# A gated state-space and dense kernel: other load order and warm-up at the start, due times from a table, two late output groups

## The chip, the cores and the metric

One core of one Trainium2 chip runs the kernel. The metric is the device time of one execution in microseconds, as the median of several runs. The profile is of one execution; its times are counted from the start of its span.

## The reference

For 2048 tokens x of 512 channels the output mixes two branches by a gate of each token: `g * a + (1 - g) * b`, where g is the sigmoid of the sum over channels of x times gate_w. Branch b is a dense pair of layers. Branch a is a long convolution whose 2048 taps come from 128 complex exponentials per channel; the reference does it with FFTs over 4096 points.

```python
dt = jnp.exp(log_dt)[:, None]
logdA, dB = dt * A, dt * Bc                       # 512 x 128, complex
P = jnp.exp(logdA[:, :, None] * l[None, None, :]) # l = 0 .. 2047
K = jnp.einsum("dn,dnl,dn->dl", Cc, P, dB).real
y = irfft(rfft(pad(u)) * rfft(pad(K)))[:2048] + u * Dskip   # branch a
h = gelu(x @ w1 + b1)                              # 512 -> 1792
b = h @ w2 + b2                                    # 1792 -> 512
out = g * a + (1 - g) * b
```

## The kernel before

The kernel has two parts, `front` and `conv`.

`front` runs four streams of tasks. **Dense**: the tokens go in 8 blocks of 256 (`xh`, `xlo`: each number as the sum of two of a shorter format, so that a product takes three matmuls: high by high, low by high, high by low). Each block meets the 1792 hidden columns in two passes of seven w1 tiles (`wh`, `wl`), so that there are 16 rounds, called NB. A hidden group (L904 to L906, 12 matmuls into `ph`) makes one hidden tile of 128; ACT applies the GELU and copies it to `hh`, DVE puts the rest into `hl`; an output group (L947 to L950, six matmuls, three where a step has one tile only) adds it to `acc`, one accumulator for each half of the block. A step is two hidden tiles, the fourth step of a round one: that is the last column of the pass. The second pass stores its result with an accumulating DMA on GpSimd's queue (L990). **Taps**: DVE and ACT make powers of the exponentials, 16 pieces in all; PE contracts each (L709, into `pk`), the first stage of a transform follows (L428), ACT copies its result to `sk` (L736), and SP stores it to `tk_d` in DRAM (L751), eight stores for four pieces. **Signal**: the same first stage for x, to `tu_d`. **Early**: loads of `tu_d` into rooms that become free (`den`, `loft`, `attic`, L474).

The tasks of all four streams go into a planner (`Plan.run`), which writes out the order: on each engine or queue the task with the smallest due time among those that are ready by its clock. A task's due time is worked out from constants such as `T_0`, `D_H`, `K_0`. Every engine then works through its rows in that order and waits at a row whose inputs are missing; the order never changes while the kernel runs.

At the start PE does eight matmuls on a zeroed tile `dm` (`warm`, L1025), spreads `b2` and `gate_w` over the partitions with one-row matmuls (`spread`, L1029), and goes on to the first hidden group. `make_dt` loads log_dt, makes its exponential and writes it to `dt_d`; `prepare` reads it back with a broadcast DMA to `dtb` for each of four channel blocks.

`conv` is the second stage: for each of 16 steps p2u and p2k (L1140) transform signal and taps, which come from `us` and from `tk_d` (L1119), DVE multiplies them, `pa` (L1179) goes back, ACT copies to `sa`, and SP stores to `t_d`. Loads of quarters of `t_d` (L1185) bring the rows together for the last transform pb (L1295, 16 tiles of 512 columns); DVE adds each to what the dense branch left in `mos` and SP stores the output. The output products of the last round, and one group of the last column of the round before (128 tokens, copied to `odd`), are kept in the list `late`; `rest` issues them behind the loop, while the quarters travel.

Of the kernel before, what the change touches and what calls it, by code (L numbers as in the profile page):

```python
# [33 lines left out]
T_0 = 36.21  # L34
T_MLP = 409.57
K_0 = 25.82
T_KG = 357.09
U_0 = 33.4
U_GAP = 11.32
LAG = 11.52  # L40
TABLE = 21.3
D_KA = 14.92
D_KP = -48.19
D_S1 = -107.61
D_EV = -129.31
D_H = -67.42
D_LO = -64.4
PS = (2, 3, 1, 2)
N_ACC, N_H, N_PK, N_PU = PS
D_SP = 5.83  # L50
MEM = (6, 2, 5)
N_LD, N_HL, N_ST = MEM
D_XS = 6.62
DOTS_AT = (0, 1, 7, 14, 15, 18, 20, 21)
N_WARM = 8
T_EARLY, T_LOFT, T_DEN = 347.49, 497.61, 268.21
Y_K, Y_U = 55.03, 39.32
W_MLP = (-0.0864, -0.0266, 0.0054)
W_KG = (-0.056, -0.0124, 0.0011)
W_U = (-0.025, -0.1189, 0.003)  # L60
D_MAG = -1.84
D_ROT = 0.71
D_CON = 2.06
D_PHA = -0.1
D_PRE = -2.18
D_XL = -29.86
D_COE = -3.15
D_OUT = -38.48
D_GW = 95.59
D_DT = -103.6  # L70
D_B2 = 15.56
N_LATE = 2
N_REST = 3
N_KEEP = 2
# [7 lines left out]
W_DVE = ((1, 0), (3, 0), (5, 0))  # L82

# [35 lines left out]
def constants():  # L119
# [14 lines left out]
    c1 = np.tile(np.stack([er, ei], 2).reshape(32, 64), (4, 1))  # L134

# [73 lines left out]
class Plan:  # L209
# [26 lines left out]
    def run(self):  # L236
# [8 lines left out]
        for _ in self.tasks:  # L245
# [23 lines left out]
            if p in ("SP", "GP"):  # L269
                dma = max(dma, at + 1.2) + t.done  # L270
                end = dma + 1.2
# [16 lines left out]
def gated_mix(  # L288
# [52 lines left out]
    def front(pool, psum, keep, attic, loft, den, pr):  # L341
# [57 lines left out]
        odd = keep.tile([P, 2, P], F32R, name="odd")  # L399
# [80 lines left out]
        def make_dt():  # L480
# [23 lines left out]
            move(2, lambda: nc.sync.dma_start(x, logdt.rearrange(shape, c=4)), D_DT, [], ["dt"])  # L504
# [3 lines left out]
            move(2, lambda: nc.sync.dma_start(dt_d.rearrange(shape, c=4), r), -200, ["dt"], ["dt_d"])  # L508
# [24 lines left out]
        def prepare(u, t, eb_k):  # L533
# [4 lines left out]
            move(600, lambda: nc.sync.dma_start(pr, prm[:, :, sl]), t - 20 if u else -97, [], ["pr"])  # L538
            move(
                200, lambda: nc.gpsimd.dma_start(dtb, dt_d[:, sl].to_broadcast([P, UW])), t - 20 if u else -97,  # L540
                ["dt_d"], ["dtb"], queue="GP",
            )
# [341 lines left out]
        def halves(i):  # L884
# [6 lines left out]
            k = i % N_HL  # L891
            return hh[k][:, 0:n], hl[k][:, 0:n], ("hh", k), ("hl", k)

        def hidden(i, t):
# [33 lines left out]
            act((0.75, 1.45)[nf - 1], gelu, t + D_H, ["b1"], [hk, ("h", q)], "gelu")  # L928
# [6 lines left out]
        def output(i, t):  # L935
# [4 lines left out]
            def products(s, a):  # L940
# [3 lines left out]
                for n, f in enumerate(fs):  # L944
# [4 lines left out]
                    stop = (j == 2 and n == 1) if b == NB - 2 and s else j == 3  # L949
# [4 lines left out]
            for s in range(2):  # L954
# [6 lines left out]
                if b == NB - 2 and s and j == 3:  # L961
                    for k, (z, key) in enumerate(((hi, hk), (lo, lk))):
                        pl.add(
                            "POOL", 0.3, lambda k=k, z=z: nc.gpsimd.tensor_copy(odd[:, k], z[:, 0, P:].bitcast(F32)),
                            t, [key], [("odd", k)],
                        )
                    late.append((2, odd[:, 0], odd[:, 1], wh[1][fs[0] % FH], wl[1][fs[0] % FH]))
# [26 lines left out]
        def dense():  # L994
# [6 lines left out]
                lambda: nc.gpsimd.dma_start(c1t, c1),  # L1001
# [32 lines left out]
            for q in range(1, N_ACC):  # L1034
# [4 lines left out]
            split_x(0, x, -50)  # L1039
            first = [  # L1040
                split_w(f, r, room[f][:, r], ("room", f, r), -50 + f + r * 1.5, (f, r) in W_DVE)
# [47 lines left out]
        while heap:  # L1089
# [3 lines left out]
            if t is not None:  # L1093
                heap.append((t, n, s))
        for t in pl.run():
# [4 lines left out]
    def conv(pool, ps, late, attic, loft, den, pr):  # L1100
# [116 lines left out]
        def rest(n):  # L1217

            while late and n:
# [3 lines left out]
                if first:  # L1223
                    tag, bufs = ("pk", 2) if s < 2 else ("pa1", 1)
# [53 lines left out]
        rest(15)  # L1278
# [114 lines left out]
```

## Time and profile before

| | us |
|---|---|
| runs shown, median (lowest to highest) | 510.12 (509.39 to 512.53) |
| profiled execution, its own time | 510.31 |
| its span | 508.3 |
| PE busy, 4792 instructions | 500.2 (98%) |
| DVE busy | 430.0 (85%) |
| ACT busy | 364.7 (72%) |
| GpSimd busy | 39.6 (8%) |
| moved by DMA | 107.60 MB, 212 GB/s on average |

The profile of one execution has a span, from the first to the last instruction, and the time of that execution stands beside it. A row of its views names line, engine, operation and tiles (output, arrow, inputs); "idle before" is the time in which the engine had nothing to do ahead of the row, and the name behind it is what ended that. Transfers are shown by the engine that issues them: SPq, POOLq and ACTq are the queues of SyncE, GpSimd and ScalarE.

### The profile page before, as it was taken

The numbers are of one execution on the slowest core, as the hardware profiler recorded it, in microseconds if no ns is written. First come the engines' busy times: TensorE is split into PE (matmuls) and PEld (weight loads), VectorE is DVE, ScalarE is ACT, GpSimd is POOL, SyncE is SP. The second block draws the span as 40 slices with busy tenths as digits, with TensorE's granted clock in tenths as the row PEclk, the third lists the DMA queues.
The fourth block names the chain that finished last, engine by engine and source line by source line (L and its number), as shares of the span: only waits on it lengthen the run. The fifth ranks groups of instructions, "written<-read, shape, count | busy, mean of one in ns | idle before, by whom it ended". The sixth has DMA issues, their size and how long they took to land.

```text
span 508.3 us, 12156 instructions
## 1 busy us (share of the span) xinstructions
PE 500.2 (98%) x4792; PEld 382.8 (75%) x4792; DVE 430.0 (85%) x814; ACT 364.7 (72%) x631; POOL 39.6 (8%) x80
## 2 busy tenths in 40 slices
PE   9999999999999999999998999999999999999996
PEld 6998788898989888788887898998898832222452
DVE  5797999999999999999998989999950188777546
ACT  5799997889999599999766998738634455565300
POOL 1000000000000000001020010120010000231100
PEclk9999999999999999999999999999999999999999
DMA  8977597732558642789594233951478899989997
GB/s 269 327 250 269 156 258 236 225 128 66 149 120 260 193 165 64 207 241 239 142 269 139 86 54 59 218 119 29 144 179 206 201 368 401 376 300 399 324 339 294
DMA packets 81552, 107.60 MB, mean 212 GB/s; under 512 B 39396, under 2 KB 43880, under 8 KB 80952
## 3 DMA queue, kind: packets, MB, share of 16 engines
q1 hardware_dynamic: 74936, 82.81, 51.6%
q0 software_dynamic: 6176, 21.80, 16.1%
q10 hardware_dynamic: 384, 2.23, 1.3%
q8 instruction: 37, 0.61, 0.5%
q14 instruction: 19, 0.16, 0.1%
HBM read 61.19 MB, written 45.62 MB: 210 GB/s over the span
## 4 chain that ended last, share of the span: by engine, by line
PE 74%; ACT 16%; DMA 4%; SPq 3%; issue 2%; DVE 1%; DVEq 0%; POOL 0%; ACTq 0%; POOLq 0%
PE pk L709 10%; PE ph L904 8%; PE acc L947 7%; PE ph L905 7%; PE ph L906 7%; PE acc L948 7%; PE acc L950 7%; PE p2u L1140 5%; PE p2k L1140 5%; PE pa L1179 3%; PE pb L1295 3%; ACT ph L921 2%; PE ph L428 2%; ACT L921 2%; SPq L751 1%
## 5 line engine op out<-in xcount | busy, mean ns | idle before, releaser
L904 PE MATMUL ph<-xh,wh 128*128 128x256 f32 x448 | 129.4, 289 | 0.5 <-ACT attic L446 0.5
L905 PE MATMUL ph<-xlo,wh 128*128 128x256 f32 x448 | 128.1, 286 | 1.5 <-issue 1.5
L906 PE MATMUL ph<-xh,wl 128*128 128x256 f32 x448 | 127.9, 285 | 0.0
L904 PEld LDWEIGHTS ph<-xh,wh 128*128 128x128 f32 x448 | 86.4, 193 | 9.3 <-issue 5.4
L905 PEld LDWEIGHTS ph<-xlo,wh 128*128 128x128 f32 x448 | 86.5, 193 | 3.5 <-issue 1.7
L906 PEld LDWEIGHTS ph<-xh,wl 128*128 128x128 f32 x448 | 86.4, 193 | 0.0
L947 PE MATMUL acc<-wh,hh 128*128 128x512 f32 x209 | 84.2, 403 | 0.0
L948 PE MATMUL acc<-wl,hh 128*128 128x512 f32 x209 | 82.2, 393 | 0.0
L950 PE MATMUL acc<-wh,hl 128*128 128x512 f32 x209 | 81.8, 392 | 0.0
L921 ACT ACTIVATE ph<-ph,b1t 128x256 f32<-128x256 f32 x112 | 50.4, 450 | 38.9 <-PE ph L906 37.1
L709 PE MATMUL pk<-y,den 128*32 128x64 f32 x2048 | 61.4, 290 | 0.0
L709 PEld LDWEIGHTS pk<-y,den 128*32 128x32 f32 x2048 | 57.2, 136 | 3.3 <-issue 1.8
L931 DVE TENSOR_TENSOR hl<-ph,hh 128x512 fp32r<-128x512 f32 (+1 forms) x62 | 38.3, 620 | 22.6 <-ACT hh L924 22.2
L947 PEld LDWEIGHTS acc<-wh,hh 128*128 128x128 f32 x209 | 39.3, 188 | 17.4 <-issue 7.8
L950 PEld LDWEIGHTS acc<-wh,hl 128*128 128x128 f32 x209 | 39.3, 188 | 8.8
L671 DVE TENSOR_TENSOR y<-y,ea 128x64 f32<-128x64 f32 (+4 forms) x80 | 45.4, 567 | 0.1
L948 PEld LDWEIGHTS acc<-wl,hh 128*128 128x128 f32 x209 | 39.3, 188 | 6.4
L516 DVE TENSOR_TENSOR loft<-den,zz 128x256 f32<-128x256 f32 (+2 forms) x48 | 37.4, 778 | 0.5
L517 DVE TENSOR_TENSOR loft<-den,zz 128x256 f32<-128x256 f32 (+2 forms) x48 | 37.3, 776 | 0.0
L1148 ACT COPY k<-p2k 128x512 f32<-128x512 f32 x32 | 18.7, 586 | 25.4 <-issue 10.2
L684 DVE TENSOR_TENSOR y<-y,loft 128x2048 f32<-128x2048 f32 x16 | 36.6, 2288 | 0.2
L924 ACT CAST hh<-ph 128x512 fp32r<-128x512 f32 (+1 forms) x62 | 33.0, 533 | 2.4 <-PE acc L948 0.2
(200 smaller groups left out, 875.0 us busy)
## 6 DMA issues: line engine op xcount, KB each, us to landing
tk_d<-sk SPq DMA_DIRECT2D x32, 256.0 KB, 5.0
t_d<-sa SPq DMA_DIRECT2D x32, 256.0 KB, 5.1
tu_d<-attic SPq DMA_DIRECT2D x40, 128.0 KB, 2.8
attic<-in_xt_dram SPq DMA_DIRECT2D x16, 256.0 KB, 5.4
xh_d<-xh SPq DMA_DIRECT2D x8, 512.0 KB, 4.5
xl_d<-xlo SPq DMA_DIRECT2D x8, 512.0 KB, 5.0
attic<-in_xs_dram SPq DMA_DIRECT2D x16, 256.0 KB, 5.3
out_dram<-io SPq DMA_DIRECT2D x16, 256.0 KB, 3.3
```

The lines of the kernel that those rows point to most:

```text
L516: vec(2 * m, lambda: vv.tensor_mul(t, a, br), due, [ka, *kb], [kt])
L671: nc.vector.tensor_mul(both(n, 64 - 3 * n, n), both(0, 64 - n, n), an)
L709: nc.tensor.matmul(pks[q][32 * j : 32 * j + 32, :, gg], x[:, r, :, ch], y[:, r, :, ch], start=(r == 0), stop=(r == 1), skip_group_check=True,)
L904: nc.tensor.matmul(p, h, xh[xk][:, d], start=(d == 0), stop=False)
L905: nc.tensor.matmul(p, h, xlo[xk][:, d], start=False, stop=False)
L906: nc.tensor.matmul(p, lo, xh[xk][:, d], start=False, stop=(d == 3))
L921: nc.scalar.activation(phs[q][:, n], phs[q][:, n], AF.Gelu_apprx_tanh, bias=b1t[:, f : f + 1])
L931: nc.vector.tensor_sub(lo, phs[q][:, 0:nf], hi.bitcast(F32))
L947: nc.tensor.matmul(a, h, wh[1][w], start=start, stop=False, skip_group_check=seeded)
L948: nc.tensor.matmul(a, h, wl[1][w], start=False, stop=False, skip_group_check=seeded)
L950: nc.tensor.matmul(a, l, wh[1][w], start=False, stop=stop, skip_group_check=seeded)
L1140: nc.tensor.matmul(out[64 * i : 64 * i + 64], w, x, start=True, stop=True)
```

## The change

Four things change together.

1. Due times: a string of numbers, one for each task, replaces the due times that the constants gave. The constants change too, but where a task has a due time the table's holds.
2. The start: SP loads the first half of x, then w1's first tile, then x's second half. log_dt comes by GpSimd's queue. The first `dtb` is no longer read back from DRAM: a new constant (`some`, beside `c1`) times dt is multiplied by ones on PE and copied by DVE. The warm-up has 12 matmuls instead of 8.
3. The last column of the last round but one goes behind the loop for both halves of the block (256 tokens). Its inputs stay in `hh` and `hl`; the GpSimd copies to `odd` go.
4. In the tail the matmuls that kept PE at work (N_KEEP, `warm`) are gone, and the last of the 16 pb tiles is done in two halves of 256 columns.

```diff
-D_KA = 14.92
+D_KA = 27.96
...
-N_WARM = 8
+N_WARM = 12
...
-N_KEEP = 2
...
+DUES = """
+2 48 1704 7 63 0 8 101 3 31 2 0 9 1 25 4 7 18 32 13 55 6 75 19 64 22 23 16 3 0 3 1 0 26 460 580 33 1539 174
...
+        for t, due in zip(pl.tasks, map(float, DUES.split()), strict=True):
+            t.due = due
         for t in pl.run():
             t.fn()
...
     c1 = np.tile(np.stack([er, ei], 2).reshape(32, 64), (4, 1))
+    some = np.arange(P)[:, None] == np.arange(P) // 4
+    c1 = np.concatenate([c1, some], 1)
...
-            move(2, lambda: nc.sync.dma_start(x, logdt.rearrange(shape, c=4)), D_DT, [], ["dt"])
+            move(2, lambda: nc.gpsimd.dma_start(x, logdt.rearrange(shape, c=4)), -300, [], ["dt"], queue="GP")
...
+            some, scaled, ones = (x4[0:32, 0, k] for k in range(3))
+            pl.add("POOL", 0.1, lambda: nc.gpsimd.memset(ones, 1.0), -190, [], ["x4"])
+            move(16, lambda: nc.gpsimd.dma_start(some, c1[0:32, 64:192]), -190, [], ["x4"], queue="GP")
...
+            mm(
+                0.4, lambda: nc.tensor.matmul(pus[1][:, 0:UW], ones, scaled, start=True, stop=True), -190,
+                ["x4"], [("pu", 1)], tiled=True,
+            )
+            vec(UW, lambda: v.tensor_copy(dtb, pus[1][:, 0:UW]), -190, [("pu", 1)], ["dtb"])
...
-                    load(xt[b, :, 2 * h : 2 * h + 2].rearrange("p a b -> p (a b)"), due)
+                    load(xt[b, :, 2 * h : 2 * h + 2].rearrange("p a b -> p (a b)"), due + 2 * h)
...
-                        -99 + f + r * 1.5, [], [("room", f, r)],
+                        -99 + f + r * D_W1 if f + r else -299, [], [("room", f, r)],
...
-                if b == NB - 2 and s and j == 3:
-                    for k, (z, key) in enumerate(((hi, hk), (lo, lk))):
...
-                    late.append((2, odd[:, 0], odd[:, 1], wh[1][fs[0] % FH], wl[1][fs[0] % FH]))
+                if b == NB - 2 and j == 3:
+                    late.append((2 + s, hi[:, 0], lo[:, 0], wh[1][fs[0] % FH], wl[1][fs[0] % FH]))
...
-        rest(15)
-        odd = pool.tile([P, D], F32, tag="v0", name="odd", bufs=2)
-        nc.scalar.mul(odd, accs[2], gate[:, 1, 13:14])
-
-        warm = ps.tile([P, D], F32, tag="pa0", name="warm", bufs=1)
-        for _ in range(N_KEEP):
-            nc.tensor.matmul(warm[0:64], mats[7][1][:, 1], zs[0], start=True, stop=True)
+        rest(16)
+        odd = [pool.tile([P, D], F32, tag=f"v{r}", name=f"odd{r}", bufs=2) for r in range(2)]
+        for r in range(2):
+            nc.scalar.mul(odd[r], accs[2 + r], gate[:, 1, 12 + r : 13 + r])
+
...
+                parts = [slice(0, D // 2), slice(D // 2, D)] if t == 15 else [slice(0, D)]
+                for cs in parts:
...
                 if m == 1 and i == 0:
-                    nc.vector.tensor_add(mos[6][:, 1], mos[6][:, 1], odd)
+                    for r in range(2):
+                        nc.vector.tensor_add(mos[6][:, r], mos[6][:, r], odd[r])
```

How the rows move is seen at three places. A number behind a name is a buffer; the lines of the changed kernel are its own.

**The start.** GpSimd before: the zeroed `dm`, the load of b2 into io_145, the ones of the spread, the load of the gate weights.

```order
L1019 MEMSET dm 128x128
L1016 DMA io_145<-in_b_dram 1x16x32
L1013 MEMSET s_106 1x128
L765 MEMSET phase 128x32
L1016 DMA io_146<-in_gw_dram 1x16x32
```

GpSimd in the changed kernel, from the same place on; x_98 holds the ones and the constant of the new broadcast, dts_149 log_dt.

```order
L571 MEMSET x_98 32x128
L1092 DMA io_144<-in_b_dram 1x16x32
L1095 MEMSET dm 128x128
L844 MEMSET phase 128x32
L1089 MEMSET s_106 1x128
L565 DMA dts_149<-in_logdt_dram 128x4
L1092 DMA io_145<-in_gw_dram 1x16x32
L572 DMA x_98<-in_c_dram 32x128
```

A memset and the load of b2 now stand ahead of dm. PE before, its first rows: warm-up, the two spreads, the first hidden group.

```order
L1025 MATMUL acc_87<-dm 128x128 x8
L1029 MATMUL acc_86<-io_145,s_106 128x512
L1029 MATMUL pu_92<-io_146,s_106 128x512
L904 MATMUL ph_88<-xh_108,wh_112 128x256
L905 MATMUL ph_88<-xlo_110,wh_112 128x256
```

PE in the changed kernel, its first rows.

```order
L1101 MATMUL acc_87<-dm 128x128 x12
L1105 MATMUL acc_86<-io_144,s_106 128x512
L985 MATMUL ph_88<-xh_108,wh_112 128x256
L986 MATMUL ph_88<-xlo_110,wh_112 128x256
L987 MATMUL ph_88<-xh_108,wl_126 128x256
```

The second spread and the new broadcast of dt (L583) stand 36 matmuls further on, behind three hidden groups:

```order
L986 MATMUL ph_90<-xlo_110,wh_116 128x256
L987 MATMUL ph_90<-xh_108,wl_130 128x256
L1105 MATMUL pu_92<-io_145,s_106 128x512
L583 MATMUL pu_93<-x_98 128x128
L985 MATMUL ph_89<-xh_108,wh_114 128x256
```

A 128-wide matmul in this format counts as two of the profile's instructions.

**The hand-over from front to conv.** SP before, from the last eight stores of sk on; den and loft are loads from tu_d, tk the first loads of `conv`.

```order
L474 DMA den<-tu_d 128x512
L751 DMA tk_d<-sk 64x16x64 x2
L474 DMA den<-tu_d 128x512
L751 DMA tk_d<-sk 64x16x64 x4
L474 DMA den<-tu_d 128x512
L751 DMA tk_d<-sk 64x16x64 x2
L474 DMA loft<-tu_d 128x512
L1119 DMA tk_4781<-tk_d 128x512
```

SP in the changed kernel at the same place.

```order
L535 DMA den<-tu_d 128x512
L830 DMA tk_d<-sk 64x16x64 x2
L535 DMA den<-tu_d 128x512
L830 DMA tk_d<-sk 64x16x64
L535 DMA loft<-tu_d 128x512
L830 DMA tk_d<-sk 64x16x64 x2
L535 DMA den<-tu_d 128x512
L830 DMA tk_d<-sk 64x16x64 x3
L1197 DMA tk_4783<-tk_d 128x512
```

Three loads stay among the stores; none stands behind them now. On PE, 141 rows of hidden and output groups (108 and 33) stand before between the last first stage and the first p2u; in the changed kernel 108 (84 and 24). ACT before, behind the copies to sk: the two results of the last round but one (io) that GpSimd's accumulating stores take.

```order
L921 ACTIVATE ph_90<-ph_90,b1t 128x256
L924 CAST hh_141<-ph_90 128x256
L977 ACTIVATE io_146<-acc_87,gate 128x512
L977 ACTIVATE io_145<-acc_86,gate 128x512
L921 ACTIVATE ph_88<-ph_88,b1t 128x256 x2
L924 CAST xh_108<-ph_88 128x512
```

ACT in the changed kernel at that place.

```order
L1005 CAST hh_141<-ph_90 128x256
L1002 ACTIVATE ph_88<-ph_88,b1t 128x256 x2
L1005 CAST xh_108<-ph_88 128x512
L1053 ACTIVATE io_145<-acc_87,gate 128x512
L1002 ACTIVATE ph_89<-ph_89,b1t 128x256 x2
L1005 CAST xh_108<-ph_89 128x512
L1053 ACTIVATE io_144<-acc_86,gate 128x512
```

Both results moved behind GELUs of the last round.

**The tail.** PE before: the last late group, the matmuls that kept it at work, the first pb tile.

```order
L1227 MATMUL acc_5485<-wh_125,odd 128x512
L1228 MATMUL acc_5485<-wl_139,odd 128x512
L1229 MATMUL acc_5485<-wh_125,odd 128x512
L1284 MATMUL warm<-z_4779,cc_5205 64x512 x2
L1295 MATMUL pb_5496<-den,g1t 64x512 x2
```

PE in the changed kernel.

```order
L1305 MATMUL acc_5487<-wh_125,hh_141 128x512
L1306 MATMUL acc_5487<-wl_139,hh_141 128x512
L1307 MATMUL acc_5487<-wh_125,hl_143 128x512
L1305 MATMUL acc_5491<-wh_125,hh_141 128x512
L1306 MATMUL acc_5491<-wl_139,hh_141 128x512
L1307 MATMUL acc_5491<-wh_125,hl_143 128x512
L1375 MATMUL pb_5501<-den,g1t 64x512 x2
```

One more late group stands there, and no matmuls of its kind to keep PE at work.

More of the change, by code (lines that the diff above doesn't have):

```diff
@@ L269, in run @@
             if p in ("SP", "GP"):
-                dma = max(dma, at + 1.2) + t.done
-                end = dma + 1.2
+                dma = max(dma, at + 1.2) + t.done * (1.5 if dma < 6.5 else 1.0)
+                end = dma + (1.2 if p == "SP" else 2.6)
                 landed[p].append(end)
@@ L537, in prepare @@
             act_due = t + D_KA
[L538 to L542, printed above, removed]
+            move(600, lambda: nc.sync.dma_start(pr, prm[:, :, sl]), t - 20 if u else D_PR, [], ["pr"])
+            if u:
+                move(
+                    200, lambda: nc.gpsimd.dma_start(dtb, dt_d[:, sl].to_broadcast([P, UW])), t - 20,
+                    ["dt_d"], ["dtb"], queue="GP",
+                )
             v = nc.vector
```

112 lines of the change are left out of this document (60 added, 52 removed), and 55 rows, old and new, of the table DUES.

## The prediction

> **What bounds the kernel now.** The sum is made against the profiled execution: its span is 508.3 us, its own time 510.31 us, so 2.0 us lie around the span; the three runs shown have a median of 510.12 us. One per cent, 5.1 us, is about what a measurement of this kernel can tell from no change. I read the page's first two parts and its chain of work first, then the waits of PE, then windows and timelines of the three places that the change touches: the start, the hand-over from the front to the convolution stage, and the tail.
>
> ```profile
> PE 500.2 (98%) x4792; PEld 382.8 (75%) x4792; DVE 430.0 (85%) x814; ACT 364.7 (72%) x631; POOL 39.6 (8%) x80
> PE   9999999999999999999998999999999999999996
> PE 74%; ACT 16%; DMA 4%; SPq 3%; issue 2%; DVE 1%; DVEq 0%; POOL 0%; ACTq 0%; POOLq 0%
> ```
>
> PE is busy in 98% of the span, and in nine tenths or more of every slice but the last, so time can only come from fewer matmuls, from a faster PE clock, or from the few places where PE waits. DVE stands second:
>
> ```profile
> 51.00:375.00 324.00, 321.31 (x3713) 278.39 (x3712) 315.92 (x601) 268.52 (x450) 22.45 (x45) 1.00 0.58 159
> ```
>
> DVE is busy for 315.92 of these 324 us: it feeds the tap stage, and a schedule that gives PE less to wait for must not ask more of DVE. The waits of PE's matmuls in the whole span are five:
>
> ```profile
> PE ph L905 <- issue: 1.5, 1, 1.5
> PE acc L1025 <- POOL dm L1019: 1.0, 1, 1.0
> PE ph L904 <- ACT attic L446: 0.5, 1, 0.5
> PE ph L428 <- ACT wh L808: 0.4, 1, 0.4
> PE ph L428 <- DVE hl L931: 0.2, 1, 0.2
> ```
>
> Without the 1.0 us of the start, 2.6 us are there to be had in the loop, and 1.5 us of them have no releaser that the profile shows.
>
> **The start.** PE runs at half its rate at first. The same matmuls, by count in two windows:
>
> ```profile
> 8.79:13.06 4.27, 4.27 (x21) 1.00 1.06 387
> 13.94:16.08 2.14, 2.14 (x21) 1.00 0.96 350
> 0.73 0.20 POOL L1019 MEMSET dm<- 128x128 f32 x1 [0.29 <-POOLq L1374]
> 0.99 3.79 PE L1025 MATMUL acc<-dm 128*128 128x128 f32 x16 [0.99 <-POOL dm L1019]
> 1.31 0.64 POOL L1016 DMA_DIRECT2D io<-in_b_dram  x1 [0.37 <-issue]
> 1.94 0.19 POOL L1013 MEMSET s<- 1x128 f32 x1
> 4.71 2.06 PE L1029 MATMUL acc<-io,s 1*128 1x512 f32 x2
> 6.57 1.91 PE L1029 MATMUL pu<-io,s 1*128 1x512 f32 x2
> 7.09 0.62 ACT L808 CAST wh<-sk 128x512 fp32r<-128x512 f32 x1 [2.05 <-DMA sk<-in_w_dram]
> 8.41 0.58 PE L904 MATMUL ph<-xh,wh 128*128 128x256 f32 x1
> ```
>
> 21 matmuls take 4.27 us before 13.06 us and 2.14 us after 13.94 us. From 8.41 us to the step between the two windows, near 13.3 us, the loop therefore loses about 2.4 us, and the full rate came after 4.9 us of dense work. The 16 warm-up matmuls (3.79 us) and the one-row matmuls behind them, which spread b2 and the gate weights, did not bring the full rate.
>
> The change issues 24 warm-up matmuls instead of 16, at the 0.213 us each that 16 in 3.4 us give: 5.1 us. But POOL now does a memset and the b2 load (0.64 us) ahead of the memset of dm on which the warm-up waits; dm takes the place that the memset behind that load has now, near 1.9 us, so the warm-up runs from about 2.2 to 7.3 us instead of from 0.99. One spread (1.9 us at half rate, 0.95 us at full) stays ahead of the first hidden group; the other goes 36 matmuls behind it. When the full rate comes decides the rest. If 4.9 us of dense work bring it, as they did above, it is there at 7.1 us, as the warm-up ends; the spread then takes 0.95 us, and the first hidden group starts at 8.2 us. If half of that work is enough (4.7 us), the rest of the warm-up goes at full rate and the group starts at 6.9 us; if the warm-up does not bring it, at 9.2 us, with half rate until about 13.3 us. I take the value that the row gives, 8.2 us. Its data come no later: w1's first piece is now the second of SP's transfers instead of the fourth. A hidden task still reads both halves of x, so "half of x" moves the loads, not the condition. On the path that is 8.41 - 8.2 = 0.2 us earlier and 2.4 us of half rate gone, less 0.95 us for the spread that came behind, 0.25 us for the new matmul that broadcasts dt (a quarter of a spread's columns), and some 0.8 us in which that matmul waits for DVE, which has a weight tile (0.7 us) and the last dt rows ahead of it: 0.6 us gained. The bounds are 2.7 us gained (6.9 us, no wait for DVE) and 2.4 us lost (9.2 us: 0.8 later, half rate 0.4 us cheaper, 1.2 us of added matmuls, the wait).
>
> [...]
>
> The earlier dt also lets DVE begin the taps sooner. That shortens DVE's chain, which is not the end's bound, and I price it at nothing as long as PE stays the busier engine.
>
> **The loop.** One output group of three matmuls leaves it for the tail. A matmul of that shape takes 0.23 us from start to start, one of a hidden group 0.12 us:
>
> ```profile
> 59.02 0.29 PE L905 MATMUL ph<-xlo,wh 128*128 128x256 f32 x1
> 59.14 0.28 PE L906 MATMUL ph<-xh,wl 128*128 128x256 f32 x1
> 382.99 0.40 PE L947 MATMUL acc<-wh,hh 128*128 128x512 f32 x1
> 383.23 0.39 PE L948 MATMUL acc<-wl,hh 128*128 128x512 f32 x1
> ```
>
> That is 0.7 us off a saturated stretch. All other instructions stay, in another order. Five output groups of the old order stand only two hidden groups (24 x 0.12 = 2.9 us) behind the hidden group whose GELU they read, one of the new; so I let 1.3 us of the 2.6 us of waits go. Bounds: all 2.6 us gone, or as much again added, since the new order was never run in this trace.
>
> **The hand-over.** Here the change costs. The taps' last first-stage products leave PE, ACT copies them to sk, SP stores them to tk_d in eight transfers, and SP loads them back as tk for the first p2k matmul:
>
> ```profile
> 382.29:402.92 20.63, 20.63 (x141) 19.11 (x141) 2.50 (x4) 9.96 (x20) 2.32 (x4) 1.00 0.84 193
> 402.92:406.41 3.49, 3.49 (x18) 1.19 (x17) 1.12 (x2) 0.95 (x3) 0.00 (x0) 1.00 0.76 214
> 382.29 2.06 ACT sk L736 x4
> 384.37 0.59 SPq L751
> 394.77 7.46 DMA tk_d<-sk
> 402.31 0.33 SPq L1119
> 406.41 4.33 PE L1140 MATMUL p2k<-tk,pr 128*64 128x512 f32 x16
> PEld p2k L1140 <- DMA tk<-tk_d: 0.4, 1, 0.4
> q0 software_dynamic: 288, 0.52, 16.3%
> ```
>
> From the first copy (382.29) to the first p2k (406.41) the transfers take 24.1 us, and PE needs as long: 20.63 us for 141 matmuls, then 3.49 us of p2u. The two end together, with a 0.4 us wait. In the new order 108 matmuls stand there, 24 hidden ones and 9 output ones fewer: 24 x 0.12 + 9 x 0.23 = 4.9 us less. PE is ready 15.7 + 3.5 = 19.2 us after the first copy. The chain of transfers is nearly the same: eight stores and three loads from tu_d (the last of the three no longer behind the stores, where it did not delay them). What differs is the two accumulating stores of the output on GpSimd's queue: they held 16.3% of the DMA time from 384 to 402.3 us, 3.0 us; in the new ACT order they follow the GELUs of the last block, so one meets the last stores and one the loads. The chain takes 21.1 us without them and 24.1 us as before; with one of two in the way I take the middle, 22.6. PE then stands still for 3.4 us (1.9 to 4.9) instead of 0.4: +3.0 us.
>
> **The tail.**
>
> ```profile
> 485.61 1.56 ACTq L1185 DMA_DIRECT2D den<-t_d  x2
> DMA to landing us min/median/max: 3.9/4.0/4.6
> 488.10 1.93 PE L1284 MATMUL warm<-z,cc 128*64 128x512 f32 x4
> 489.65 3.81 PE L1295 MATMUL pb<-den,g1t 128*64 128x512 f32 x16
> 492.47 0.68 DVE L1302 TENSOR_TENSOR loft<-loft,odd 128x512 f32<-128x512 f32 x1
> 496.25 6.76 DVE L1305 SCALAR_TENSOR_TENSOR loft<-pb,gate,loft 128x512 f32<-128x512 f32 x8
> 503.12 1.74 DVE L1305 SCALAR_TENSOR_TENSOR attic<-pb,gate,attic 128x512 f32<-128x512 f32 x3
> ```
>
> The first pb matmul starts at 489.65 us, as the quarter that ACT issued at 485.61 us lands (3.9 us). The warm matmuls (488.10, 1.93 us) fill that wait. The change takes them out and puts the 0.7 us of matmuls into the same wait: nothing moves, because the transfer ends it; should the transfer come earlier than PE, the 0.7 us would be back. The second add of odd costs DVE 0.68 us, but DVE needs 0.77 us for a tile (3.07 us for four) where PE's pace is 0.845 (6.76 us for eight), and gains 0.075 us on each of the fourteen tiles left, 1.0 us in all. The last tile in halves lets DVE begin its first half sooner, yet DVE still has the tile before it (0.77 of the 1.74 us): 0.1 us gained, at most 0.4.
>
> **The sum.** -0.6 - 0.7 - 1.3 + 3.0 - 0.1 = +0.3 us. Span 508.6 us, time 510.6 us: **no change** by this working.
>
> **The rivals.** *The transfers are in time.* If the eight stores and the loads keep up with the shorter stretch (fewer packets beside them than I count), the 3.0 us fall away and with them the old 0.4 us: 507.2 us, and with the best start (2.1 more), a loop without waits (1.3) and the last tile's 0.3 us 503.5 us. For it: one store's issue takes SP only 0.59 us when nothing is queued. Against it: 7.46 us from the last store's issue to its landing, with DMA as the chain's only holder.
>
> *PE goes cold in the hand-over (slower).* Its wait there is one gap, and the windows at the start show a PE that had to work 4.9 us before it got the full rate. If such a gap takes the rate away again, the same 4.9 us at half rate cost 2.4 us on top: 513.0 us, with the wait at its upper bound (1.5 more) 514.5 us, and with the cold start (3.0 more) 517.5 us. It decides from the gap at which the rate falls, which no row here shows, for PE never waits over 1.5 us; against it is that my gap is short. [...]
>
> *The new order stalls PE.* A table of due times for every task may put a matmul group ahead of its GELU or its weights: as much waiting again as now, +2.6 instead of -1.3, gives 514.5 us. Against it are the longer distances counted above.
>
> *It does not do what it says*: the longer warm-up does not bring the full rate, and the first group starts at 9.2 us. Then 0.6 gained becomes 2.4 lost, 513.6 us.
>
> **How the numbers follow.** No change by the sum 0.48; transfers in time 0.25; PE cold 0.12; new stalls 0.08; no early rate 0.07. The predicted time is that of the sum, 510.6. From 503.5 (the best of the second case) to 514.5 (both slow ones at their bounds) about 8 in 10 are held; I give 504.0 to 515.0. Faster by over 1% (below 505.0) needs the second case with a good start or an unstalled loop, 0.15 of its 0.25, and 0.04 of the first: 0.19. Slower by over 1% (above 515.2) needs PE cold with a cold start, stalls beside the full wait, or a cold start beside it: 0.07 + 0.04 + 0.03 = 0.14. The rest, 0.67, is within 1%.
>
> **What would show it.** Start: the first hidden matmul near 8.2 us, 0.12 us apart from the outset, and a gap ahead of the dt matmul. Loop: the waits of PE below 2.6 us. Hand-over: PE idle between p2u and p2k for 2 to 5 us, released by the load of tk; if PE is idle for less than 1 us there, the main cost is wrong. Tail: pb's first matmul still released by the load of den. I am wrong if the rate at the start is half up to 13 us, if DVE holds the last tap chunk back, or if the loop's stalls differ by more than 2.6 us.

## The result, and the profile after

The changed kernel takes 512.93 us (median of 19 runs, 511.05 to 517.81) against 510.12 us (19 runs, 508.9 to 512.53) before: ratio 1.0056, 95% interval 1.0039 to 1.0073. That is slower by 0.6%, inside the 1% that was called no change and inside the range, 2.3 us above the forecast of 510.6. The profiled execution has a span of 511.1 us, 2.8 us more than before.

The row of the engines and PE's row of the 40 slices, after the change:

```profile
PE 498.3 (98%) x4802; PEld 379.6 (74%) x4802; DVE 430.4 (84%) x817; ACT 363.6 (71%) x631; POOL 39.5 (8%) x80
PE   8999999999999999999999999999999699999995
```

PE does 1.9 us less and the span is longer: one slice, the 32nd, has fallen to 6 tenths. The waits of PE say which place that is:

```profile
PE p2k L1218 <- DMA tk<-tk_d: 3.9, 1, 3.9
PE acc L1101 <- POOL phase L844: 2.2, 1, 2.2
PE pb L1375 <- DMA den<-t_d: 0.8, 1, 0.8
PE p2k L1218 <- ACT k L1226: 0.4, 1, 0.4
PE pu L583 <- DVE x L575: 0.2, 1, 0.2
PE p2u L1218 <- DVE hl L1012: 0.2, 1, 0.2
```

No wait of the loop is left, and the hand-over has one of 3.9 us. Its rows in PE's timeline (start, duration, line, operation):

```profile
398.90 1.94 PE L1218 MATMUL p2u<-den,pr 128*64 128x512 f32 x8
...
406.82 5.97 PE L1218 MATMUL p2k<-tk,pr 128*64 128x512 f32 x16 [3.85 <-DMA tk<-tk_d]
...
415.04 1.09 PE L1257 MATMUL pa<-v,pr 64*64 64x512 f32 x8
```

And four windows around it (width, PE, PEld, DVE, ACT and POOL busy, granted clock, DMA share, GB/s):

```profile
400.71:404.12 3.41, 2.06 (x10) 0.49 (x8) 0.26 (x1) 0.00 (x0) 0.00 (x0) 1.00 0.92 167
404.12:407.53 3.41, 0.71 (x3) 0.30 (x5) 0.00 (x0) 0.00 (x0) 0.00 (x0) 1.00 0.66 191
407.53:410.94 3.41, 3.41 (x10) 1.21 (x10) 0.69 (x1) 0.59 (x1) 0.00 (x0) 0.50 1.01 314
410.94:414.36 3.42, 3.03 (x15) 0.76 (x13) 2.67 (x5) 2.48 (x5) 0.00 (x0) 1.00 1.05 382
```

PE stands still for 3.85 us before the first p2k matmul. The window that holds most of the gap has 0.71 us of work, and in the next one, 3.41 us long, PE is busy throughout at a granted clock of 0.50. The sixteen p2k matmuls take 5.97 us instead of 4.33. So the gap is paid twice, as waiting and as a half-rate window behind it: 3.41 us at half rate do the work of 1.7 us.

By stages, the two profiled executions differ so:

| stage, and where its ends are read | before | after | difference |
|---|---|---|---|
| span's start to the first p2u | 402.92 | 398.90 | -4.0 |
| first p2u to first p2k | 3.49 | 7.92 | +4.4 |
| first p2k to first pa | 6.25 | 8.22 | +2.0 |
| first pa to first pb | 77.0 | 76.9 | -0.1 |
| first pb to the span's end | 18.6 | 19.1 | +0.5 |

(Before, the first pa matmul started at 412.66 us.) The 4.0 us that PE gains ahead of p2u are given back in the next row, and the stretch with the half-rate window is 2.0 us longer (1.7 us for the window; p2k's later matmuls also wait 0.4 us for ACT). The loop in a window of the same width, before and then after:

```profile
51.00:380.00 329.00, 326.31 (x3848) 283.02 (x3847) 316.89 (x603) 269.61 (x452) 22.45 (x45) 1.00 0.59 160
```

```profile
51.00:380.00 329.00, 329.00 (x3869) 285.08 (x3871) 316.20 (x603) 265.94 (x447) 22.35 (x45) 1.00 0.57 160
8.20:11.60 3.40, 3.40 (x24) 2.66 (x23) 1.72 (x6) 2.52 (x6) 0.00 (x0) 1.00 1.06 389
```

PE's busy time rises from 326.31 to 329.00 of 329.00 us: all 2.7 us of waiting are gone. (The last row is of the start. The rate there is read from the matmuls, for the granted clock is given as 1.00 from 2.20 to 7.70 us too: the spread, which ends just ahead of the hidden group, takes 1.37 us, where it takes 1.9 to 2.1 us at half rate (the kernel before) and 1.12 at full (the second spread of this execution, at 13.40 us), so the full rate came near 8.2 us; before, it came near 13.3.) DVE has 316 to 317 us in both, and its last tap piece ends nearly where it did, before and then after:

```profile
373.89 1.21 DVE L695 TENSOR_TENSOR y<-y,loft 128x1024 f32<-128x1024 f32 x1
```

```profile
374.25 1.22 DVE L774 TENSOR_TENSOR y<-y,loft 128x1024 f32<-128x1024 f32 x1
```

That is 375.10 us before and 375.47 after. DVE could not finish sooner: a few rows earlier it waited 2.0 us for a contraction of PE, which came late in the new order.

```profile
366.71 0.17 DVE L804 TENSOR_TENSOR pk<-pk,dm 128x8 f32<-128x8 f32 x1 [2.01 <-PE pk L788]
```

Before, the same row (L725) stood at 364.33 us, with a wait of 0.27. One row of the start and one of the tail, after:

```profile
8.94 0.39 PE L985 MATMUL ph<-xh,wh 128*128 128x256 f32 x1
491.98 1.51 PE L1375 MATMUL pb<-den,g1t 128*64 128x512 f32 x6 [0.76 <-DMA den<-t_d]
```

The first hidden group starts 0.5 us later than before (8.94 instead of 8.41 us), at full rate, and pb still waits for its load. As for the hand-over: PE got ahead, the taps did not, and the first p2k needs the taps: the first copy to sk went from 382.29 to 383.25 us, and the first p2k only from 406.41 to 406.82.

### The profile page after: what moved, and what is told of

It is laid out like the page before. It is cut to its first block, busy times and chain, and to the rows that moved or that the text cites. A ratio compares the mean times of both kernels' runs of the same rounds, so it can differ in the third digit from the quotient of the medians.

```text
span 511.1 us, 12182 instructions
## 1 busy us (share of the span) xinstructions
PE 498.3 (98%) x4802; PEld 379.6 (74%) x4802; DVE 430.4 (84%) x817; ACT 363.6 (71%) x631; POOL 39.5 (8%) x80
## 4 chain that ended last, share of the span: by engine, by line
PE 90%; DMA 4%; SPq 2%; ACT 1%; issue 1%; DVE 1%; POOL 0%; DVEq 0%; ACTq 0%; POOLq 0%
PE pk L788 12%; PE acc L1028 10%; PE ph L985 10%; PE ph L987 10%; PE ph L986 10%; PE acc L1029 9%; PE acc L1031 9%; PE p2k L1218 6%; PE p2u L1218 5%; PE ph L489 3%; PE pa L1257 3%; PE pb L1375 3%; DMA tk_d<-sk 2%; SPq L830 1%; PE acc L1101 1%
## 5 line engine op out<-in xcount | busy, mean ns | idle before, releaser
L985 PE MATMUL ph<-xh,wh 128*128 128x256 f32 x448 | 127.4, 284 | 0.0
L986 PE MATMUL ph<-xlo,wh 128*128 128x256 f32 x448 | 126.7, 283 | 0.0
L985 PEld LDWEIGHTS ph<-xh,wh 128*128 128x128 f32 x448 | 85.1, 190 | 6.7 <-issue 4.6
L986 PEld LDWEIGHTS ph<-xlo,wh 128*128 128x128 f32 x448 | 85.1, 190 | 2.0
L987 PEld LDWEIGHTS ph<-xh,wl 128*128 128x128 f32 x448 | 85.1, 190 | 0.0
L1028 PEld LDWEIGHTS acc<-wh,hh 128*128 128x128 f32 x208 | 39.1, 188 | 18.6 <-issue 8.6
```

Source lines behind the costliest of these rows:

```text
L985: nc.tensor.matmul(p, h, xh[xk][:, d], start=(d == 0), stop=False)
L986: nc.tensor.matmul(p, h, xlo[xk][:, d], start=False, stop=False)
L987: nc.tensor.matmul(p, lo, xh[xk][:, d], start=False, stop=(d == 3))
L1028: nc.tensor.matmul(a, h, wh[1][w], start=start, stop=False, skip_group_check=seeded)
```

## The experiments

After the result the theory was: the first p2k is set by the taps' last contraction and the transfers behind it, so PE's gain ahead of it only opens a gap, and the gap costs a half-rate window as well. The rival was that the slow stretch behind the gap comes from the transfers beside it. Each run below is timed against the kernel before on the same chip, whose median was 509.8 to 510.1 us.

### The gap filled

```diff
         signal(1)
+        warm = ps.tile([P, D], F32, tag="pa0", name="warm", bufs=1)
+        for _ in range(16):  # 8 and 4 in the other two runs
+            nc.tensor.matmul(warm[0:64], mats[0][0][0][:, 0], us[0], start=True, stop=True)
         taps(0)
```

> The changed kernel with 16 more matmuls, on data already there, between the last p2u and the first p2k matmul, where the trace shows PE idle for 3.85 us and then the granted clock at 0.5 for 3.4 us. 16 x 0.22 = 3.5 us fit into the gap. Theory (the gap costs twice, once as waiting and once as a half-rate window behind it): no half-rate window, the stretch from the first p2k to the first inverse matmul falls from 8.2 to about 6.3 us as before the change, time 511.0 instead of 512.9 us. Rival (the slow first p2k matmuls come from the transfers beside them, not from the gap): the stretch stays at 8.2 us, time 512.9 us or up to 0.3 more.

> The same with 8 matmuls, which leave some 2.1 us of idle PE instead of 3.85. It tells from which gap on the rate falls. If 2 us of idle PE are too few: as with 16, 511.0 us and no half-rate window. If 2 us are enough to lose the rate: 512.9 us and the window is there.

Sixteen gave 519.86 us (ratio 1.0195, 1.0160 to 1.0229), eight 514.19 us (ratio 1.0082, 1.0054 to 1.0110). I had mis-sized the filling: one of these matmuls takes 0.86 us and not 0.22. They have two records of 0.43 us each; p2k's take 0.27 us a record (sixteen in 4.33 us before). They go to the two halves of the output in turn and mine all went to one half; whether that makes the difference was not tried.

```profile
402.67 6.60 PE L1325 MATMUL warm<-den,pr 128*64 128x512 f32 x15
```

This is the row of the eight, at two records each (one more stands behind it). They hold PE until 409.2 us, 2.4 us too long, and sixteen far longer. Both say nothing of the gap's length, but no half-rate window follows in either profile: the last fifteen of the sixteen p2k matmuls take 4.05 us in both. So the run was made again with a size that fits:

> The changed kernel with 4 more matmuls between the last p2u and the first p2k matmul. In the run with 8 of them one took 0.86 us and all 6.9 us, 2.4 us more than the gap of 3.85 us holds (first p2k at 409.2 instead of 406.8 us), while the granted clock stayed at 1.00; 4 take 3.4 us and fit. Theory (the gap costs its length and a half-rate window of 1.9 us behind it): first p2k where it was, no half-rate window, 511.0 us instead of 512.9. Rival (the window is not worth what the p2k rows say, its matmuls would have waited for ACT or the transfers anyway): 512.5 to 513 us.

It gave 510.96 us (509.79 to 513.35; ratio 1.0026, 1.0006 to 1.0045), the forecast of the theory. The profiled execution:

```profile
405.35 5.01 PE L1218 MATMUL p2k<-tk,pr 128*64 128x512 f32 x16
```

```profile
405.30:408.70 3.40, 3.40 (x12) 1.25 (x13) 0.84 (x2) 1.17 (x2) 0.00 (x0) 1.00 1.04 304
```

The matmuls compute nothing that is used, the transfers are as busy beside p2k as they were (DMA share 1.04, 1.01 in the half-rate window of the change), and the half-rate window is gone. The mean granted clock of the twelve executions is 0.997 to 1.000, against 0.988 to 0.997 in the nineteen of the change. So the transfers do not explain the half rate, and the rival falls. The size is less sharp: the time fell by 2.0 us between the medians and by 1.5 us by the ratios (1.0056 and 1.0026). In the profile the stretch from the first p2k to the first pa fell from 8.22 to 6.91 us, not to the 6.3 that I expected: the sixteen p2k matmuls take 5.01 us there, 4.33 before the change, and these rows do not show why; and the first p2k came 1.5 us earlier, which is not the window's doing. A second control is the run with 16 warm-up matmuls below: a gap of 3.64 us, no half-rate window, and 6.59 us for the stretch.

### The taps' end moved forward

```diff
-        for t in pl.run():
+        order = pl.run()
+        for what, past in ((1331, 1361), (1382, 1423), (1398, 1476), (1438, 1479)):
+            a, b = order.index(pl.tasks[what]), order.index(pl.tasks[past])
+            order.insert(b, order.pop(a))
+        for t in order:
             t.fn()
```

Tasks 1331, 1382, 1398 and 1438 are output groups of six matmuls; 1361, 1423 and 1476 are the last three contractions and 1479 is the last first-stage product. The first run had only the first three pairs.

> The changed kernel with three output groups (1.4 us each) moved behind the last three contractions of the taps, which they hold up; no work is added or left out. Theory (the first p2k is set by the taps' end plus the transfers, and PE's gain ahead of it is lost in the gap): the copies to sk and the first p2k come 2 to 3 us earlier, PE's gap shrinks from 3.85 to about 1 us, the half-rate window is gone, time 508 to 509 us. Rival (the transfers are bound by something that does not move with the copies, or DVE takes the time back): first p2k where it was, 512.9 us; if the contractions now make PE wait for DVE, up to 514 us.

512.53 us (510.48 to 514.61; ratio 1.0049, 1.0020 to 1.0078): the copies came 1.0 us earlier, the first p2k 0.4, and the gap was 4.4 us. Two output groups still stood between the last contraction and the product. With the fourth pair:

> The changed kernel with the three output groups behind the last three contractions as in e2_early, and the one that stood between the last contraction and the first-stage product behind that product too. In e2_early the last copy to s came 2.3 us earlier but the copies to sk only 1.0 us, because two output groups stood ahead of the product. Theory: copies to sk near 380.6 instead of 383.3 us, first p2k near 404.2, PE's gap 1.2 us and no half-rate window: 508 to 509 us. Rival (the transfers do not move with the copies: in e2_early 1.0 us of earlier copies brought 0.4 us): first p2k near 405.7, gap 2.7 us, a half-rate window in some executions, 511 to 512 us.

509.34 us (507.75 to 510.86; ratio 0.9984, 0.9964 to 1.0004).

```profile
381.04 0.59 ACT L815 COPY sk<-pu 128x512 f32<-128x512 f32 x1 [1.87 <-PE pu L489]
```

```profile
403.82 2.79 PE L1223 MATMUL p2k<-tk,pr 128*64 128x512 f32 x8 [1.73 <-DMA tk<-tk_d]
```

The copies come 2.2 us earlier, the first p2k 3.0, and the gap of 1.7 us is followed by no half-rate window: the sixteen p2k matmuls take 5.3 us behind it, 5.97 in the change. DVE's last tap piece ends at 373.27 instead of 375.47 us, so the taps themselves came sooner once PE's contractions stood ahead of the output groups. No work was taken out: the 3.6 us between the medians come from the order of four groups.

### The transfers relieved

The chain of work of the changed kernel between the copies and the first p2k (start, duration, what; most of the stores and the gaps of under 0.1 us are left out):

```profile
383.25 2.05 ACT sk L815 x4
...
386.72 1.33 SPq L535
...
389.54 0.69 SPq L535
...
392.49 1.49 SPq L535
...
395.96 8.06 DMA tk_d<-sk
404.16 2.61 DMA tk<-tk_d
```

SP's queue sets the pace of the eight stores; three loads of tu_d (L535) stand in it for 3.5 us, and the last store needs 8.06 us to land. Two accumulating stores of the output run beside it. One run left these out:

```diff
-                            lambda n=n, r=r: nc.gpsimd.dma_start(out[n], io[r], accum_op=ALU.add),
+                            lambda n=n, r=r: n < 12 and nc.gpsimd.dma_start(out[n], io[r], accum_op=ALU.add),
```

> The changed kernel without its last two accumulating stores of the output (tiles 12 and 13 of the output lack their first half), which run beside the stores and loads of the taps' products. Theory of the prediction (they take 1.5 to 3.0 us of the transfers' time): the first copy to the first p2k takes 20.5 to 22 us instead of 23.6, PE's gap is 0.8 to 2.3 us, time 508 to 511.4 us, the lower end if the half-rate window goes too. Rival (SP's issue sets the chain's pace and they run beside it): 23.6 us as before, 512.9 us.

509.07 us (507.69 to 513.11; ratio 0.9988, 0.9963 to 1.0013). Its profiled execution had a granted clock of 0.95 from the start to the end, so only the transfers are read from it: first copy to first p2k 21.3 us instead of 23.6, between these rows of its chain and of PE.

```profile
383.63 2.05 ACT sk L815 x4
```

```profile
404.90 4.61 PE L1218 MATMUL p2k<-tk,pr 128*64 128x512 f32 x16 [1.44 <-DMA tk<-tk_d]
```

The last store lands in 5.82 us instead of 8.06. By these two profiles the two stores cost the chain 2.3 us, inside the prediction's 1.5 to 3.0; in three other profiles that have them there (the two of the section above and that with 16 warm-up matmuls) the chain takes 22.8 to 24.1 us, so the 2.3 is good to about a microsecond. Holding them back instead (io in the pool that lives on, four buffers of sa instead of six, and ahead of the third product's signal):

```diff
+            if s == 2:
+                tiny = pool.tile([1, 1], F32, name="tiny", bufs=1)
+                nc.gpsimd.tensor_copy(tiny, prod[2][1][0:1, 0:1])
+                for r in range(2):
+                    nc.gpsimd.dma_start(out[12 + r], io[r], accum_op=ALU.add)
```

> The changed kernel with its last two accumulating stores of the output held back until the third product of the convolution stage, with the io tiles kept for it (sa has four buffers instead of six to make the room). Nothing is left out. Theory (two of these stores cost the chain of transfers 2.3 us and, with the gap above some 2 us, a half-rate window): as without them, first copy to first p2k 21.3 us, gap near 1.5 us, 509 us. Rival (the transfers of the convolution stage have no room for them either, or four sa buffers hold PE): the time comes back behind 415 us, 511 to 513 us.

511.59 us (510.32 to 514.73; ratio 1.0028, 1.0006 to 1.0050). The limit of some 2 us in that expectation was an estimate, and no run shows it: a gap of 3.64 us was followed by no half-rate window (last section). The chain took 21.1 us and the gap shrank to 1.4 us as forecast, but the rival came true as well (three of PE's waits):

```profile
PE p2k L1218 <- ACT f L401: 2.7, 3, 1.4
PE pb L1380 <- DMA den<-t_d: 2.1, 1, 2.1
PE p2k L1218 <- DMA tk<-tk_d: 1.4, 1, 1.4
```

The first pa to the first pb took 81.7 us instead of 76.9. Whether the moved stores or the fewer sa buffers made these waits, this run cannot tell. The other way is to move the three loads, which nobody needs yet:

```diff
-                    256, lambda n=n: nc.sync.dma_start(us[n], tu_d[k0_order()[n]]), due,
+                    256, lambda n=n: n not in (6, 7, 26) and nc.sync.dma_start(us[n], tu_d[k0_order()[n]]), due,
...
             fetch(n)
+            if n == 5:
+                for k in (6, 7):
+                    nc.sync.dma_start(us[k], tu_d[ko[k]])
...
+        nc.sync.dma_start(us[26], tu_d[ko[26]])
         nc.sync.dma_start(g1t, g1.rearrange("p (b k) -> p b k", b=2))
```

> The changed kernel with three loads of tu_d (tiles 6, 7 and 26 of the signal), which SP issues between the eight stores of the taps' products, moved behind the sixth and the last load of those products; nothing is left out, and their first reader comes two modules of the convolution stage later. They hold SP's queue for 1.33 + 0.69 + 1.49 = 3.5 us. Theory (the chain from the copies to the first p2k is bound by SP's queue and the transfers in it): first copy to first p2k 20 us instead of 23.6, PE's gap below 0.5 us, no half-rate window: 512.9 - 3.5 - 1.9 = 507.5 us. Rival (the last stores' landing is set by the two accumulating stores beside them): 22 to 22.5 us, gap 2 to 2.5 us, 511 us.

> The changed kernel with both moves: the three loads behind, as in e8_defer, and the output groups behind the last contractions, as in e5_early2 (which gave 509.3 us with a gap of 1.7 us). Theory: PE never waits between p2u and the first p2k, so nothing but PE's own work bounds the hand-over: 507 us, faster than before the change (510.1) by 0.6%. Rival (the loads that were moved come late in the convolution stage, or DMA has no room for them there): 509 us or more, with waits of PE behind 410 us.

The loads alone: 509.58 us (507.77 to 512.83; ratio 0.9998, 0.9976 to 1.0020), which lies between theory and rival. The last rows of its chain:

```profile
392.81 5.45 DMA tk_d<-sk
398.58 4.43 DMA tk<-tk_d
403.06 1.07 PE p2k L1218 x2
```

The last store was issued 10.8 us after the first copy (382.03) instead of 12.7 and landed in 5.45 instead of 8.06 us, but the load of tk then took 4.43 instead of 2.61 us. It came 5.6 us earlier than in the changed kernel (398.58 instead of 404.16 us), where GpSimd's queue had 1.5% of the DMA engines' time during the load. That it met the accumulating stores now and was slower for that is my guess, and was not tried by itself. First copy to first p2k: 21.0 us, gap 1.3 us. With both moves the time is **508.06 us** (507.15 to 510.52), ratio 0.9974 to the kernel before, interval 0.9955 to 0.9993: the only version whose interval lies below the kernel before, and by little. The wait of its p2k and p2k's first row:

```profile
PE p2k L1223 <- DMA tk<-tk_d: 0.2, 1, 0.2
```

```profile
401.64 1.07 PE L1223 MATMUL p2k<-tk,pr 128*64 128x512 f32 x2
```

PE goes from p2u to p2k without a gap and waits 0.2 us inside it. Only here does the total fall below that of the kernel before; it is 1 us less than I expected.

### Two parts of the change by themselves

The warm-up, first by the constant alone (`N_WARM = 8`), then with the order kept (`range(N_WARM - 4)` in the loop that issues the matmuls):

> The changed kernel with 16 warm-up matmuls instead of 24, all else alike. Theory of the prediction (the longer warm-up brings the full rate 5 us sooner, worth some 2 us of PE's time at the start) together with the new one (the first p2k is set by the taps and the transfers, which do not wait for PE's start): the full rate comes later in the records and p2u up to 2 us later, but the first p2k stays near 406.8 us, the gap shrinks by what the start loses, and the time stays at 512.9 us or falls to 511 where the gap gets short enough to keep the rate. Rival (what the start loses is lost at the end): 514 to 515 us.

> The changed kernel with its order kept word for word, but 16 of the 24 warm-up matmuls issued (in e4_warm8 the smaller number also reordered the whole program, which cost 26 us). Theory of the prediction for the start: the first hidden group comes up to 1.7 us sooner, but the full rate comes up to 5 us later in the records; PE reaches the first p2u up to 2 us later. New theory for its price (the first p2k is set by the taps' last contraction and the transfers): the first p2k moves by less than 0.5 us, PE's gap shrinks by what the start loses, and the time stays at 512.9 us, or falls to 511 where the gap gets short enough to keep the rate. Rival (a loss at the start is a loss at the end): 514 to 515 us.

The first gave 539.38 us (538.52 to 540.90; ratio 1.0579, 1.0549 to 1.0609). It says nothing of warm-up: the planner reckons the warm-up's length from this constant, and with other start times it orders the whole program anew from the same due table. The waits of PE's matmuls had thirteen rows instead of six, 26 us in all. The second gave 512.38 us (510.95 to 514.86; ratio 1.0066, 1.0040 to 1.0092), the time of the change with 24.

```profile
398.65 1.94 PE L1218 MATMUL p2u<-den,pr 128*64 128x512 f32 x8
406.35 4.44 PE L1218 MATMUL p2k<-tk,pr 128*64 128x512 f32 x16 [3.64 <-DMA tk<-tk_d]
```

The first p2k moved by 0.5 us and the gap by 0.2. PE did not even reach p2u later than with 24; the eight extra warm-up matmuls are not worth anything that these runs show. As the start lost nothing, this run does not test what a loss there would cost.

The late column, on the kernel before: `b == NB - 2 and j == 3` sends both halves of w2's last column behind the loop (accumulators 2 and 3, two adds of odd, no warm matmuls), and the rest stays.

> The kernel before, with the third part of the change alone: w2's last column for 256 tokens instead of 128 behind the loop, without the warm matmuls there. The rest of its order stays. The output group that goes stands 43 rows behind the last first-stage product, between the first copy to sk and the first p2k. Term of the prediction: 0.7 us faster, 509.4 us. New theory (in that stretch the transfers set the first p2k): the first p2k stays near 406.4, the wait ahead of it grows from 0.4 to about 1.1 us, pb's start and the time stay: 510.1 us.

510.27 us against 509.78 (ratio 1.0012, 0.9992 to 1.0032). The interval leaves out a gain of 0.7 us, as the new theory has it. Its profile did not show the wait that I expected, though:

```profile
400.05 3.65 PE L1136 MATMUL p2u<-den,pr 128*64 128x512 f32 x16
403.67 5.04 PE L1136 MATMUL p2k<-tk,pr 128*64 128x512 f32 x16
```

The first copy stood at 380.10 us, so the transfers took 23.6 instead of 24.1 us in that execution and ended with p2u. One execution cannot resolve half a microsecond there. The due table by itself, the new loads at the start and the halved pb tile were not run alone.

## Why the prediction came out as it did

The number held, and the likeliest case did not: the time that came, 512.93, is that of the rival *PE goes cold in the hand-over*, 513.0 us, to which I gave 0.12. The mechanism is that rival's; that it agrees to 0.1 us is luck, for its 2.4 us were too much for the window and the tail came out 0.5 us too long.

- **Start, -0.6:** the first p2u came 4.0 us earlier; without the loop's 2.7 and the group's 0.7 us, 0.6 are left for the start, as forecast. The pieces differ, so the agreement is partly luck: the full rate is there near 8.2 us, where I had it at 7.1, the 24 warm-up matmuls take 5.5 us for my 5.1, the first hidden matmul starts at 8.94 instead of 8.2 us, and the dt matmul waits 0.2 instead of 0.8 us.
- **Output group, -0.7:** right for PE's work and worth nothing at the end. The group stood behind the taps' last product, where the transfers set the first p2k; my +3.0 took it back, and the late column alone brought nothing.
- **Loop, -1.3:** mis-sized, 2.7 us went. I let the new order remove half of the waits; it removed them all. It made no difference, because the next wait took it. I also priced DVE's chain at nothing; it is where the taps end, and the new order made it wait 2.0 us for PE.
- **Hand-over, +3.0:** the mechanism is right. The chain took 23.6 us for my 22.6, the gap is 3.85 us for my 3.4 (1.9 to 4.9). My terms put the first p2k at 406.41 - 2.6 + 3.0 = 406.8 us, and it is at 406.82. Errors cancel there: p2u came 1.4 us earlier than the terms say; the gap grew by 0.45 us and p2u by 0.6 (4.1 us with a wait of 0.2 for hl, instead of 3.5), and the 0.4 us that I took off as the old wait was a wait of weight loads, in which PE did not stand still. The copies and the transfers, not PE, set that point, so p2u's lead could only turn into waiting; but from the copies at 383.25 us a chain of my 22.6 us would have put the first p2k at 405.9 us, so the hit on 406.8 is luck.
- **The step that failed** is the sentence "against it is that my gap is short". I knew no row for the gap from which the rate falls, set 3.4 us as short, and left the half-rate window out of the sum. The stretch behind the gap is 2.0 us longer, 1.7 of it the half-rate window, where the rival priced 2.4 for 4.9 us at half rate; filling the gap brings back 1.5 to 2.0. The gap of 3.85 us was followed by the loss of the rate; one of 3.64 us in another execution was not (last section), so no run gives the length from which it falls.
- **Tail, -0.1:** pb still waits for the load of den (0.76 us), and 10.9 us lie between the last pa and the first pb as before, so the late matmuls are free as I said. From pb to the end it is 0.5 us more (19.1 us). Of the ten later profiles with this tail at the full clock, eight have 18.9 to 19.9 us there and two 18.3 and 18.6, which is what the two with the old tail have (18.3 and 18.6). So the new tail is probably some 0.4 us longer, where I forecast 0.1 shorter; what makes it so was not looked into.

## What to carry to other kernels

Before you add gains up, ask for each which event at the next hand-over it moves: a gain on the busiest engine is worth nothing if the next stage starts on another engine's last result and a chain of transfers. Here a gap of 3.85 us on TensorE cost its length and was followed by 3.41 us at a granted clock of 0.50. That gap could be closed to 0.2 us by order alone: by putting work that nobody waits for behind the last producer, and loads that nobody needs yet behind the stores that somebody does. Neither move alone made the kernel clearly faster than before; both together did. A table of due times belongs to the exact program it was found for; change a constant that the planner reads, and measure nothing but the new order.

## What the runs showed of the hardware

The length of a gap alone does not tell whether the rate is lost. In the change the granted clock falls to 0.50 at 407.53 us and is back at 1.00 from 410.94 us, 3.41 us later; in the 3.41 us ahead of the fall PE has 0.71 us of work. With 16 warm-up matmuls the gap was 3.64 us, almost that of the change, and the execution that was profiled lost nothing:

```profile
401.08:404.49 3.41, 1.63 (x8) 0.29 (x4) 0.00 (x0) 0.00 (x0) 0.00 (x0) 1.00 0.65 112
404.49:407.90 3.41, 1.55 (x6) 0.66 (x7) 0.00 (x0) 0.00 (x0) 0.00 (x0) 1.00 0.84 288
407.90:411.31 3.41, 3.13 (x14) 0.95 (x13) 2.42 (x4) 2.87 (x6) 0.00 (x0) 1.00 1.05 360
```

I chose the edges of these rows, in widths of 3.41 us; nothing in the records marks an edge there. The gap lies across the edge at 404.49 us, with 1.63 and 1.55 us of work in the two rows beside it. With the gap of 4.4 us (the first three groups moved) the 3.41 us ahead of the fall were empty, and half rate lasted 6.83 us, in the first half of which PE had only 2.49 us of work:

```profile
402.05:405.46 3.41, 0.00 (x0) 0.00 (x0) 0.00 (x0) 0.00 (x0) 0.00 (x0) 1.00 0.45 95
405.46:408.87 3.41, 2.49 (x6) 1.34 (x8) 0.00 (x0) 0.00 (x0) 0.00 (x0) 0.50 0.95 333
408.87:412.29 3.42, 3.42 (x11) 1.31 (x9) 1.64 (x3) 1.99 (x4) 0.00 (x0) 0.50 1.05 366
```

So gaps of 3.64, 3.85 and 4.41 us were followed by 0, 3.41 and 6.83 us at half rate, in one profiled execution each. Why the first lost nothing is not shown. Of the 19 runs of the change the slowest, 517.81 us, has the lowest mean granted clock, 0.988 against 0.993 to 0.997 in all but one of the others (0.990, in a run of 513.10 us).

The rate also fell without such a gap. At the start of the kernel with the late column alone, 3.41 us in which PE was busy for 2.87 us, 2.2 us of them with the two spreads' one-row matmuls, and waited for nothing longer than 0.22 us, were followed by 3.42 us at half rate:

```profile
4.57:7.98 3.41, 2.87 (x8) 0.91 (x7) 2.28 (x8) 1.58 (x4) 0.00 (x0) 1.00 0.88 293
7.98:11.40 3.42, 3.42 (x16) 3.42 (x17) 2.98 (x10) 3.02 (x5) 0.00 (x0) 0.50 1.07 371
```

```profile
4.67 1.12 PE L1025 MATMUL acc<-io,s 1*128 1x512 f32 x2
5.93 1.12 PE L1025 MATMUL pu<-io,s 1*128 1x512 f32 x2
```

The execution with 16 warm-up matmuls shows the same at its start, with 1.1 us of one-row matmuls in the first of these rows and no wait above 0.34 us:

```profile
5.13:8.54 3.41, 2.76 (x14) 1.61 (x13) 2.48 (x8) 2.00 (x4) 0.00 (x0) 1.00 0.96 309
8.54:11.96 3.42, 3.42 (x18) 3.42 (x17) 2.77 (x8) 2.04 (x5) 0.00 (x0) 0.50 1.06 392
```

Whether the one-row matmuls play a part in this was not tried. Without them the first of these rows still has some 1.6 us of work, as much as each of the two rows beside the gap of 3.64 us, so PE's busy time alone does not tell when the rate falls.
